# A cached two-layer decode block: the products of each pass in columns, the first pair's q made first, and new tables

## The chip, the cores and the metric

The kernel runs on one core of one Trainium2 chip. The metric is the device time of one execution in microseconds (us), lower is better. A core has a matrix engine (PE, with its weight loads listed apart as PEld), a vector engine (DVE), a scalar engine (ACT), a general engine (POOL) and a sync engine (SP), which here only issues loads. SBUF is the on-chip memory; PSUM holds the results of PE.

## What is computed

Batch 4, one token each, width D = 512, 32 query heads on 8 key and value heads of 128 elements, caches of 4096 positions in bfloat16. Two equal layers run one after the other on the same caches and weights:

```python
def A(x):                                    # attention on the cache
    q = (x @ wq).reshape(B, 1, 32, 128)...
    scores = einsum("bhqd,bhkd->bhqk", q, k) * 128 ** -0.5
    o = einsum("bhqk,bhkd->bhqd", softmax(scores), v)
    return o.reshape(B, 1, 32 * 128) @ wo
def F(x):                                    # gated feed-forward, 1792 wide
    return (sigmoid(x @ w_gate) * (x @ w_up)) @ w_down
x = x + A(layernorm(x)); x = x + F(layernorm(x))
x = x + A(layernorm(x)); x = x + F(layernorm(x))
```

K and V of one batch entry and one head are 1 MB each, so both caches are 64 MB, and each layer needs all of them.

## The kernel before

**Units and pairs.** A unit is one layer, one batch entry and one key head: 64 units. Two neighbouring heads make a pair; `ORDER` (L125) lists the 32 pairs as three digits, layer, batch entry, pair of heads. A batch entry may enter layer 1 as soon as its layer 0 is through, so pairs of both layers are mixed.

**Slots and kept units.** A K or V of a unit takes one of 12 slots in SBUF of 1 MB; the four parts of wq become slots 13 to 16 when q is needed no more (`yield_wq`, L979). `KEPT` (L124) names, for each batch entry, the heads whose K, and behind the slash those whose V, stay in their slots from layer 0 to layer 1; those are loaded once, all others twice. Before, 29 are kept: 19 K and 10 V.

**Loads.** `LOADS` (L129) is the order of all loads: k and v of the next unit, o, g, u, d parts of the four weights besides wq. `pump` (L344) issues them on SP's queue, in that order, each when a slot is free; the new load waits for the last reader of the slot. A K is read last by its scores, a V by its product, unless it is kept.

**Steps.** `PROGRAM` (L133) is the order in which everything else is issued, a letter a step, written out in full. Per pair: T, t, u turn K on DVE in place, whole or by quarters (`k_turn`, L985); b puts q into a block-diagonal tile `qz` (`q_blocks`, L704, four copies on POOL out of `qs`); s and z score the two units on PE (`scores`, L996); m, p, n find the maximum (DVE, PE, DVE); e is exp on ACT; P turns the probabilities on PE; C and D copy them out of PSUM on ACT; h, r, i make the sums; a multiplies by V on PE (`pv`, L1165), o normalises on DVE, w applies wo, and f, F, l turn its row.

**The pass.** The dots of the program are the steps of `pass_steps` (L958), four times 17, one pass for each batch entry between its layers: layernorm, gate and up, down, layernorm, q of layer 1. Before, gate, up and q are made as rows: one column of x is the stationary operand and up to 512 columns of the weights move past it, in four strips of the array, so that the result lies in one row per strip. Gate goes through tanh on ACT as 128x512 (L828), up is multiplied on DVE as 128x512 (L853), `h_turn` (L860) brings the row into columns with four matmuls and a copy; `down` (L929) has its weights stationary. q's two halves go through a 128x512 operation on ACT (L901) and one on DVE (L907), `q_turn` (L912) brings them into columns, `q_spread` (L677) spreads them over the array's rows with 16 matmuls and a copy on ACT into `qs`. Only then may the batch entry's first pair of layer 1 take its b.

The final feed-forward, behind the last pair, has all four entries together, with weights stationary in gate and up.

Of the kernel before, what the change touches and what calls it, by code (L numbers as in the profile page):

```python
# [6 lines left out]
ACTF = mybir.ActivationFunctionType  # L7
# [116 lines left out]
KEPT = ["012345/23", "0145/01", "067/0167", "234567/36"]  # L124
ORDER = """  # L125
002 000 001 003 011 013 101 012 010 102 100 021 022 020 023 110 112 030 103 120 123 032 033 031 113
# [7 lines left out]
stzwbmtpnwett szbwtmh srwPtCTipDaazabnmeaPotthw sttprznwbCmDieaaaawhPoDritpxwttCnetaw szhwbPamTpan  # L134
saDeorwtfuiCaPhuFaazwwalDowmr.Cp.ne.h.i..rP....aa...aaCoiD..aa..tubwu szawxbmapneT
sPhoriCzDaTamabapun szePbmph szoCunbDreiamtahaaor spxPwTinzCwmbDfaewpFawlawanxothPwrit
s.zCehrDmbptta...atun s..uPt.atz..eaoCb. sDhia.raaam..ptoPtCDzwwnei.m.aabwt.paaPohrtCw.un
szimuDabape sznhwbrmPaapoew sizCDPnaamhaaeruhoCipwaDPwaaafubCnDrFloiweahaTawa.oT
sr.PDiw.zmC.apwtbwwna.t.aehao.ri sPCDT...zaawmapne....PahtuoriC.auD.a.baw sztb smpnwzatbmehroTP
spnDziCeaaTPamThprb snaoCzDeiaThamwPabaorittC sDapwznaeaatPmbhptor  # L140
swDiCneaaPhaTarCozmwwiDfapbaFlanaowTeh.rTP sDC.i..z.mb.paa.an.te.thwar.PTo
s..izm..tCD.wa.wpn.eaabaht szboPDCmprneiw szmbapa sThwPnzarteba szoihCDPbmptnaaCraae
sTDhwoiPmpaanCerawaDohziPmaCaparDneaowwihfPFaaClarawDXaoaiNYawa
# [3 lines left out]
def bass_interleave_layers__gqa_block_cached__glu_gated_glu__decode_kernel(  # L147
# [556 lines left out]
    def q_blocks(g):  # L704
        _, b, u = seq[2 * g]
        for a in range(4):
            ps = slice(32 * a, 32 * a + 32)
            S.inst(
                "pool",
                (lambda a, ps: lambda e: e.tensor_copy(  # L710
                    qz_sb[ps, :, :, a, :],
                    qs_sb[b][ps, :, u * REP:(u + 2) * REP].rearrange("p t (u r) -> p u t r", r=REP),
                ))(a, ps),
                reads=[f"qs{b}", "pf"],
                writes=[f"qz{a}"],
            )
# [91 lines left out]
    def gate_row(part):  # L808
        fns = []
        wv = wg_sb.rearrange("p k (f d) -> p k f d", d=2 * P)  # L810
        for k in range(2 * part, 2 * part + 2):
            for st in range(4):
                nt = (KW - st + 3) // 4
                fns.append(
                    (lambda k, st, nt: lambda e: e.matmul(
                        M_ps[0][32 * st:32 * st + 1, 0:nt * 2 * P],
                        lhsT=xc_bf[:, k, 0:1],
                        rhs=wv[:, k, bass.ds(st, nt, step=4), :],
                        start=(k == 0),
                        stop=(k == KD - 1),  # L820
                    ))(k, st, nt)
                )
        if part == 0:
            S.group("pe", fns, reads=["xcb"] + wkeys["wg"], writes=["M0"])
            return
        S.last_write["M0"] = S.group("pe", fns, reads=["xcb"] + wkeys["wg"])
        act(
            lambda e: e.activation(t_row[:, :], M_ps[0][:, :], ACTF.Tanh, scale=rs[:, 0:1]),  # L828
            reads=["rs", "M0"],
            writes=ROW,  # L830
        )

    def up_row(part):
        fns = []
        wv = wu_sb.rearrange("p k (f d) -> p k f d", d=2 * P)
        for k in range(2 * part, 2 * part + 2):
            for st in range(4):
                nt = (KW - st + 3) // 4
                fns.append(
                    (lambda k, st, nt: lambda e: e.matmul(  # L840
                        M_ps[1][32 * st:32 * st + 1, 0:nt * 2 * P],
                        lhsT=xc_bf[:, k, 0:1],
                        rhs=wv[:, k, bass.ds(st, nt, step=4), :],
                        start=(k == 0),
                        stop=(k == KD - 1),
                    ))(k, st, nt)
                )
        if part == 0:
            S.group("pe", fns, reads=["xcb"] + wkeys["wu"], writes=["M1"])
            return  # L850
        S.last_write["M1"] = S.group("pe", fns, reads=["xcb"] + wkeys["wu"])
        dve(
            lambda e: e.scalar_tensor_tensor(  # L853
                out=row_sb[:, 0, :], in0=t_row[:, :], scalar=1.0, in1=M_ps[1][:, :], op0=ALU.add, op1=ALU.mult
            ),
            reads=["rc", "rd", "rb", "M1"],
            writes=["ra"],
        )

    def h_turn():  # L860
        fns = []
        for t in range(2):
            for e_ in range(2):
                fns.append(
                    (lambda t, e_: lambda e: e.matmul(
                        M_ps[0][:, bass.ds(8 * t + e_, 4, step=2)],
                        lhsT=row_sb[:, 0, bass.ds(2 * P * t + e_, P, step=2)],
                        rhs=strips,
                        start=True,
                        stop=True,  # L870
                    ))(t, e_)
                )
        S.group("pe", fns, reads=["ra"] + IDENT, writes=["M0"])
        dve(
            lambda e: e.tensor_copy(hT_bf[:, :, 0], M_ps[0][:, 0:KF]),
            reads=["M0"],
            writes=["rc", "rd"],
        )

    def q_row(h, part):  # L880
        fns = []
        wv = wq_sb.rearrange("p k (h j s d) -> p k h j s d", h=2, j=4, s=4)
        for k in range(2 * part, 2 * part + 2):
            for st in range(4):
                fns.append(
                    (lambda k, st: lambda e: e.matmul(  # L886
                        M_ps[h][32 * st:32 * st + 1, :],
                        lhsT=xc_bf[:, k, 0:1],
                        rhs=wv[:, k, h, :, st, :],
                        start=(k == 0),  # L890
                        stop=(k == KD - 1),
                    ))(k, st)
                )
        rd = ["xcb"] + [f"wq{k}" for k in range(KD)]
        if part == 0:
            S.group("pe", fns, reads=rd, writes=[f"M{h}"])
            return
        S.last_write[f"M{h}"] = S.group("pe", fns, reads=rd)
        if h == 0:
            act(  # L900
                lambda e: e.activation(row_sb[:, 0, :], M_ps[0][:, :], ACTF.Copy, scale=rs[:, 0:1]),  # L901
                reads=["M0", "rs"],
                writes=["ra"],
            )
        else:
            dve(
                lambda e: e.tensor_scalar(row_sb[:, 1, :], M_ps[1][:, :], rs[:, 0:1], None, op0=ALU.mult),  # L907
                reads=["M1", "rs"],
                writes=["rc", "rd", "rb"],
            )  # L910

    def q_turn():  # L912
        fns = []
        for h in range(2):
            for j in range(4):
                n = 4 * (4 * h + j)
                fns.append(
                    (lambda h, j, n: lambda e: e.matmul(
                        M_ps[0][:, n:n + 4], lhsT=row_sb[:, h, j * P:(j + 1) * P], rhs=strips, start=True, stop=True
                    ))(h, j, n)  # L920
                )
        S.group("pe", fns, reads=ROW + IDENT, writes=["M0"])
        dve(
            lambda e: e.tensor_copy(qT_sb[:, 0:HQ], M_ps[0][:, 0:HQ]),
            reads=["M0"],
            writes=["rb"],
        )
# [30 lines left out]
    def pass_steps(b0):  # L958
        return [
            lambda: ln_a(b0, 1, 0.5 * RS),  # L960
            lambda: ln_b(1),
            lambda: gate_row(0),
            lambda: gate_row(1),
            lambda: up_row(0),
            lambda: up_row(1),
            h_turn,
# [469 lines left out]

    ln_a(0, Bn, RS)
# [10 lines left out]
    last = {}  # L1448
    for g in range(NP):
        last[seq[2 * g][:2]] = g  # L1450
    firsts = {}
    for g in reversed(range(NP)):
        firsts[seq[2 * g][:2]] = g
    renewed = set()
    turns = [i for i in range(NU) if loaded("k", i)][2:]
# [6 lines left out]
    def step(c):  # L1462
# [18 lines left out]
        elif c == ".":  # L1481
# [3 lines left out]
            if len(passes) == 2:  # L1485
                yield_wq()
        else:
            g = count[c]
            count[c] += 1
            if c == "b":  # L1490
                l, b, _ = seq[2 * g]
                assert count["z"] == g and (l == 0 or b in renewed)
# [171 lines left out]
```

## Time and profile before

| | us |
|---|---|
| runs: median (lowest to highest, 3 runs) | 306.57 (305.49 to 306.58) |
| the profiled execution | 307.3 |
| its span, first to last instruction | 305.4 |
| output issued in it at | 303.1 |
| mean granted clock of PE | 0.70 |

The loads in the profiled execution:

| load | issues | KB each | median us from issue to landing |
|---|---|---|---|
| V to slots 1 to 12 | 50, and 2 halves | 1024, 512 | 9.5, 23.8 |
| K to slots 1 to 12 | 43 | 1024 | 9.7 |
| V, K to the parts of wq | 3, 2 | 1024 | 10.2, 13.0 |
| wq | 2 | 2048 | 9.9 |
| wo | 8 | 512 | 17.1 |
| gate, up | 2, 2 | 896 | 12.3, 14.2 |
| down | 1, 1 | 1024, 768 | 14.6, 16.1 |

A row of the groups by line reads: line, engine, operation, output<-input, its shape, how often; then busy time in all and mean ns of one; then the idle time of the engine just ahead of it and what ended most of it. Matmuls overlap, so busy time divided by the count is the spacing, and the mean the length of one. A row of the stages has start and end, length, and busy time of PE, PEld, DVE, ACT and POOL with counts, then the granted clock (1 is full), the share of the DMA engines and GB/s. A row of the queue's waits has who waited, for whom, the total, the times and the longest. L12 is line 12 of the kernel; from line 704 on the changed kernel has other line numbers.

### The profile page before, as it was taken

Reading aid. Unit: us, or ns where it says so; the run is one execution under the profiler, and the core shown is the slowest. Engines: PE = TensorE matmul, PEld = TensorE weight load, DVE = VectorE, ACT = ScalarE, POOL = GpSimd, SP = SyncE. Lnnn points to the kernel's source line nnn. Section 1 sums busy time; section 2 is a strip of 40 time slices with the busy share of each in tenths; the row PEclk is TensorE's granted clock in tenths of the full one; section 3 lists DMA queues with packets and bytes.
Section 4 is the critical chain, followed back from the end, with each engine's and each line's share of the span. In section 5 each row is a group of like instructions: output and inputs, shape, how many; then the busy total and the mean of one; then the engine's idle time right before and its main releaser. Section 6 shows DMA issues by size and latency. Waiting matters only on the chain. (4 is left out here: it accounts for less than half of the span.)

```text
span 305.4 us, 11330 instructions
## 1 busy us (share of the span) xinstructions
PE 221.1 (72%) x4872; PEld 150.0 (49%) x4872; DVE 192.6 (63%) x419; ACT 117.6 (39%) x413; POOL 40.3 (13%) x205
## 2 busy tenths in 40 slices
PE   1222451854789788898886789977889798897986
PEld 1221131532645455646555656544647564564675
DVE  6334857377133786786863488649995878484343
ACT  1001142244223245814445634315555424555600
POOL 0001111110000221111121110022211010330000
PEclk9999999999995555756679555565555577555555
DMA  7999999999999999999999999999999999999900
GB/s 292 420 400 418 408 406 391 422 418 407 397 406 417 421 420 414 415 418 421 414 411 412 415 361 422 417 398 420 422 418 417 410 381 384 420 423 420 397 36 3
DMA packets 20505, 118.43 MB, mean 388 GB/s; under 512 B 1892, under 2 KB 5992, under 8 KB 7656
## 3 DMA queue, kind: packets, MB, share of 16 engines
q1 hardware_dynamic: 20432, 117.71, 94.8%
q8 instruction: 38, 0.62, 0.8%
q14 instruction: 11, 0.09, 0.1%
q10 hardware_dynamic: 24, 0.01, 0.0%
HBM read 117.71 MB, written 0.00 MB: 385 GB/s over the span
## 5 line engine op out<-in xcount | busy, mean ns | idle before, releaser
L994 DVE STREAM_TRANSPOSE slot<-slot 128x1024 f32<-128x1024 f32 (+2 forms) x74 | 103.8, 1405 | 19.3 <-DMA slot<-in_A_k_cache_dram 17.1
L1134 ACT ACTIVATE pT<-PT 32x128 bf16<-32x128 f32 x232 | 62.0, 267 | 56.5 <-PE PT L1082 31.8
L1010 PE MATMUL S_ps<-slot,qz 128*16 128x256 bf16 x992 | 61.2, 397 | 14.6 <-DVE slot L994 7.1
L1180 PEld LDWEIGHTS O_ps<-pT,slot 128*128 128x128 bf16 x1792 | 53.2, 103 | 36.7 <-ACT pT L1134 20.9
L1180 PE MATMUL O_ps<-pT,slot 128*128 128x4 bf16 x1792 | 58.3, 166 | 17.3 <-ACT pT L1134 5.9
L1064 ACT ACTIVATE wide<-S_ps,small 128x256 bf16<-128x256 f32 x64 | 30.3, 474 | 56.1 <-DVE small L1057 32.0
L710 POOL COPY qz<-qs 32x32 bf16<-32x32 bf16 x128 | 26.0, 203 | 137.3 <-PE S_ps L1010 71.3
L1010 PEld LDWEIGHTS S_ps<-slot,qz 128*16 128x16 bf16 x992 | 27.0, 112 | 33.8 <-DVE slot L994 9.4
L1027 DVE TENSOR_REDUCE small<-S_ps 128x2 bf16<-128x512 f32 x32 | 21.7, 678 | 16.8 <-PE S_ps L1010 16.0
L1082 PE MATMUL PT<-ident_bf,wide 128*128 128x64 bf16 (+1 forms) x288 | 18.5, 226 | 3.3 <-ACT wide L1064 2.2
L1082 PEld LDWEIGHTS PT<-ident_bf,wide 128*128 128x128 bf16 x288 | 15.1, 121 | 10.2 <-ACT wide L1064 4.6
L1050 DVE SCALAR_TENSOR_TENSOR O_ps<-O_ps,small,wide 128x128 f32<-128x128 f32 x32 | 10.9, 340 | 11.8 <-PE O_ps L1036 9.8
L1237 PE MATMUL AC<-wo,oT 128*1 128x512 bf16 x96 | 11.2, 560 | 7.0 <-DMA wo<-in_A_wo_dram 6.7
L1093 POOL CAST small<-small 128x2 bf16<-128x2 f32 x32 | 5.9, 184 | 79.0 <-ACT wide L1064 71.9
L1211 DVE TENSOR_TENSOR oT<-O_ps,small 128x8 bf16<-128x8 f32 (+1 forms) x32 | 5.4, 167 | 16.1 <-PE O_ps L1180 14.3
L886 PE MATMUL M_ps<-wq,small 128*1 128x512 bf16 x128 | 13.4, 562 | 0.0
L1064 ACT ACTIVATION_READ_ACCUMULATOR wide<-S_ps,small 128x1 f32 x64 | 12.3, 193 | 0.0
L1057 DVE TENSOR_REDUCE small<-O_ps 128x2 f32<-128x128 f32 x32 | 9.3, 292 | 3.3 <-DVE O_ps L1050 0.5
L695 ACT ACTIVATE qs<-M_ps 128x128 bf16<-128x128 f32 x8 | 1.9, 280 | 24.2 <-PE M_ps L684 24.1
L901 ACT ACTIVATE t_row<-M_ps,small 128x512 bf16<-128x512 f32 x4 | 2.7, 687 | 19.6 <-PE M_ps L886 19.6
L1036 PE MATMUL O_ps<-ident_bf,small 128*128 128x64 bf16 x64 | 8.6, 225 | 2.0 <-DVE small L1027 1.6
L1148 PE MATMUL O_ps<-small 128*128 128x4 bf16 x124 | 7.8, 168 | 2.8 <-POOL small L1096 2.6
(144 smaller groups left out, 210.6 us busy)
## 6 DMA issues: line engine op xcount, KB each, us to landing
slot<-in_A_v_cache_dram SPq DMA_DIRECT2D x50, 1024.0 KB, 9.5
slot<-in_A_k_cache_dram SPq DMA_DIRECT2D x43, 1024.0 KB, 9.7
wq<-in_A_wq_dram SPq DMA_DIRECT2D x2, 2048.0 KB, 9.9
wo<-in_A_wo_dram SPq DMA_DIRECT2D x8, 512.0 KB, 17.1
wq<-in_A_v_cache_dram SPq DMA_DIRECT2D x3, 1024.0 KB, 10.2
wq<-in_A_k_cache_dram SPq DMA_DIRECT2D x2, 1024.0 KB, 13.0
wu<-in_B_w_up_dram SPq DMA_DIRECT2D x2, 896.0 KB, 14.2
wg<-in_B_w_gate_dram SPq DMA_DIRECT2D x2, 896.0 KB, 12.3
```

The costliest lines, as they stand in the source:

```text
L710: (lambda a, ps: lambda e: e.tensor_copy(qz_sb[ps, :, :, a, :], qs_sb[b][ps, :, u * REP:(u + 2) * REP].rearrange("p t (u r) -> p u t r", r ...
L886: (lambda k, st: lambda e: e.matmul(M_ps[h][32 * st:32 * st + 1, :], lhsT=xc_bf[:, k, 0:1], rhs=wv[:, k, h, :, st, :], start=(k == 0), sto ...
L994: dve(lambda e: e.transpose(kf, kf), writes=[f"s{st}"])
L1010: (lambda t, b2, e_, c, x1, r0: lambda e: e.matmul(S_ps[p][r0:r0 + 4 * REP, half], lhsT=qz_sb[:, part, t, :, :].rearrange("p a r -> p (a r)"),
L1027: dve(lambda e: e.tensor_reduce(rm_bf, S_ps[p].rearrange("p (u n) -> p u n", u=2), AX.X, ALU.max), reads=[f"S{p}"], writes=["rmb"])
L1050: lambda e: e.scalar_tensor_tensor(out=shifted, in0=maxima, scalar=rowk_f, in1=mask_f.rearrange("p n w -> p (n w)").unsqueeze(1).broadcast ...
L1057: dve(lambda e: e.tensor_reduce(nm_sb, shifted, AX.X, ALU.min), reads=[f"O{n}"], writes=["nm"])
L1064: (lambda u, half: lambda e: e.activation(pe_sb[:, half], S_ps[p][:, half], ACTF.Exp, bias=nm_sb[:, u:u + 1], scale=exp_scale, accum_out=s ...
L1082: (lambda w, a0, a1, c0: lambda e: e.matmul(PT[:, c0:c0 + 16 * (a1 - a0)], lhsT=wide_sb[:, NV + 64 * w:NV + 64 * w + P], rhs=valid_bf[:, : ...
L1134: (lambda dst, frm: lambda e: e.activation(dst, frm, ACTF.Copy))(dst, frm),
L1180: (lambda n, x, c, j: lambda e: e.matmul(bank[:, ul * REP:(ul + 1) * REP], lhsT=vv[:, x * JG + c * 4 + j, :], rhs=pT[:, x % 2, ul, j, 2 * ...
L1237: (lambda r, h, i: lambda e: e.matmul(AC[32 * r:32 * r + 1, :], lhsT=oT_sb[:, h, own_column:own_column + 1], rhs=wo_sb[:, h, :], start=(j ...
```

## The change

- `KEPT` names 32 units instead of 29: 20 K and 12 V. `LOADS` has 110 entries instead of 113, with another order; `ORDER` and `PROGRAM` are other tables of the same kind.
- Gate and up of a pass are made in columns, 56 matmuls each with a 128x128 block of the weights stationary and one column of x moving, as `down` was already. Tanh and the product then work on 14 columns (128x14), and `h_turn` is gone; an empty step stands in its place.
- q of a pass is made in columns too, 128 matmuls in four groups of 32 (8 heads, two key heads each). The group of the entry's first pair of layer 1 comes first, is scaled on DVE, spread by 16 matmuls, and the pair's step b copies it from PSUM into `qz`, two of four copies on DVE and two on ACT. The other three groups follow, then the scale and spread of all heads into `qs`, from which later pairs take their blocks on POOL as before. So there are two spreads a pass, and each pass still has 17 steps.
- wq's parts become slots when one step of the last pass is left, not two; that is behind the last q matmul in both.

```diff
-KEPT = ["012345/23", "0145/01", "067/0167", "234567/36"]
+KEPT = ["012345/023", "0145/015", "0167/0167", "234567/67"]
 ORDER = """
-002 000 001 003 011 013 101 012 010 102 100 021 022 020 023 110 112 030 103 120 123 032 033 031 113
+003 001 002 000 011 013 101 012 010 100 102 021 022 110 023 020 112 103 030 123 032 120 031 033 113
 111 121 133 131 130 132 122
 """
 LOADS = """
-vkookkvkkk ovkovkoovk ukvkvkvogo guddvvvkvk kkvkvvvkvk kvkkvvvkvk vvvvvvkkkv vkvvkvvkvk kkvkkkkvvv
-vkkvvkkkvv kvvkkvvvvv vvv
+kokkkkookk ouvkkkoovo vvkkvovvvg gdudvvkkvv kkvvkvvkvk kvvkkvvkvv kvkvkvvvkk vvkvvkkkvv kkkvvkvvkk
+vkkvvkvvkv kvkvvvvvvv
 """
...
     def q_blocks(g):
-        _, b, u = seq[2 * g]
+        l, b, u = seq[2 * g]
+        if l == 1 and g == firsts[1, b]:
+            frm = M_ps[1][:, 0:NT4 * HQ].rearrange("p (t h) -> p t h", t=NT4)[:, :, u * REP:(u + 2) * REP]
+            frm = frm.rearrange("p t (u r) -> p u t r", r=REP)
+            for a in (0, 2, 1, 3):
+                ps = slice(32 * a, 32 * a + 32)
+                if a < 2:
+                    dve(
+                        (lambda a, ps: lambda e: e.tensor_copy(qz_sb[ps, :, :, a, :], frm[ps]))(a, ps),
...
+                else:
+                    act(
+                        (lambda a, ps: lambda e: e.activation(qz_sb[ps, :, :, a, :], frm[ps], ACTF.Copy))(a, ps),
...
+            return
...
+    def inner_columns(w_sb, M, mk, wk, part):
         fns = []
+        for fc in range(KW * part, KW * part + KW):
+            for k in range(KD):
                 fns.append(
+                    (lambda fc, k: lambda e: e.matmul(
+                        M[:, 64 + fc:65 + fc],
+                        lhsT=w_sb[:, k, bass.ds(fc // 2 * 2 * P + fc % 2, P, step=2)],
+                        rhs=xc_bf[:, k, 0:1],
...
+    def gate_columns(part):
+        inner_columns(wg_sb, M_ps[0], "M0", "wg", part)
+        if part == 1:
+            act(
+                lambda e: e.activation(t_sb[:, 0:KF], M_ps[0][:, 64:64 + KF], ACTF.Tanh, scale=rs[:, 0:1]),
...
+    def up_columns(part):
+        inner_columns(wu_sb, M_ps[1], "M1", "wu", part)
+        if part == 1:
+            dve(
+                lambda e: e.scalar_tensor_tensor(
+                    out=hT_bf[:, :, 0], in0=t_sb[:, 0:KF], scalar=1.0, in1=M_ps[1][:, 64:64 + KF],
...
+    def q_columns(n, first):
         fns = []
+        for h in range(2 * REP * n, 2 * REP * (n + 1)):
+            for k in range(KD):
                 fns.append(
+                    (lambda h, k: lambda e: e.matmul(
+                        M_ps[0][:, h:h + 1],
+                        lhsT=wq_sb[:, k, h * DH:(h + 1) * DH],
+                        rhs=xc_bf[:, k, 0:1],
...
+    def q_scale(h0, h1):
+        dve(
+            lambda e: e.tensor_scalar(qT_sb[:, h0:h1], M_ps[0][:, h0:h1], rs[:, 0:1], None, op0=ALU.mult),
...
+    def spread_of(h0, h1):
...
+                        M_ps[1][32 * a:32 * a + 32, t * HQ + h0:t * HQ + h1],
+                        lhsT=ident_bf[:, bass.ds(c0, 32, step=2)],
+                        rhs=qT_sb[:, h0:h1],
...
     def pass_steps(b0):
...
             lambda: ln_a(b0, 1, 0.5 * RS),
             lambda: ln_b(1),
-            lambda: gate_row(0),
-            lambda: gate_row(1),
-            lambda: up_row(0),
-            lambda: up_row(1),
-            h_turn,
+            lambda: gate_columns(0),
+            lambda: gate_columns(1),
+            lambda: up_columns(0),
+            lambda: up_columns(1),
+            lambda: None,
             lambda: down(b0, 1, 0),
             lambda: down(b0, 1, 1),
             lambda: ln_a(b0, 1, RS),
             lambda: ln_b(1),
-            lambda: q_row(0, 0),
-            lambda: q_row(0, 1),
-            lambda: q_row(1, 0),
-            lambda: q_row(1, 1),
-            q_turn,
-            lambda: (q_spread(b0, 1), renewed.add(b0)),
+            first_q,
+            first_spread,
+            lambda: q_columns(rest[0], True),
+            lambda: q_columns(rest[1], False),
+            last_q,
+            all_spread,
         ]
...
-            if len(passes) == 2:
+            if len(passes) == 1:
                 yield_wq()
```

More of the change, by code (lines that the diff above doesn't have):

```diff
@@ L844, in up_row @@
                         start=(k == 0),
                         stop=(k == KD - 1),
-                    ))(k, st, nt)
+                    ))(h, k)
                 )
[L848 to L851, printed above, removed]
-        dve(
[L853 to L857, printed above, removed]
+        rd = ["xcb"] + [f"wq{k}" for k in range(KD)]
@@ L869, in h_turn @@
                         start=True,
                         stop=True,
-                    ))(t, e_)
+                    ))(t, a, 64 * b2 + e_)
                 )
[L873 to L927, printed above, removed]
+        S.group("pe", fns, reads=["rb"] + IDENT, writes=["M1"])
@@ L1435, in last_unit @@
         parts(sq_hl, sq_sb.rearrange("p k b -> p (k b)"), ["rd"], "rb")
+    last = {}
+    for g in range(NP):
+        last[seq[2 * g][:2]] = g
+    firsts = {}
+    for g in reversed(range(NP)):
+        firsts[seq[2 * g][:2]] = g
     ln_a(0, Bn, RS)
```

107 lines of the change are left out of this document (56 added, 51 removed).

## The prediction

> **What bounds the kernel now.** I read the page first, for how full the transfers are and when they end.
>
> ```profile
> span 305.4 us, 11330 instructions
> PE 221.1 (72%) x4872; PEld 150.0 (49%) x4872; DVE 192.6 (63%) x419; ACT 117.6 (39%) x413; POOL 40.3 (13%) x205
> ...
> DMA  7999999999999999999999999999999999999900
> GB/s 292 420 400 418 408 406 391 422 418 407 397 406 417 421 420 414 415 418 421 414 411 412 415 361 422 417 398 420 422 418 417 410 381 384 420 423 420 397 36 3
> ...
> q1 hardware_dynamic: 20432, 117.71, 94.8%
> q8 instruction: 38, 0.62, 0.8%
> ```
>
> The DMA engines are busy in 38 of 40 slices; no compute engine is over 72%. The span is one stream of 117.71 MB, a short start and a tail. To see where the stream is not full, I then read the stages:
>
> ```profile
> 10.00:90.00 80.00, 37.88 (x796) 24.62 (x797) 41.62 (x70) 19.93 (x72) 7.38 (x37) 1.00 1.03 408
> 90.00:170.00 80.00, 66.93 (x1500) 44.55 (x1497) 54.33 (x122) 37.40 (x132) 14.23 (x71) 0.64 1.01 416
> 170.00:180.00 10.00, 7.56 (x202) 6.62 (x200) 5.95 (x11) 3.93 (x14) 0.61 (x3) 0.50 0.93 371
> 180.00:240.00 60.00, 51.86 (x1099) 34.43 (x1096) 45.13 (x84) 29.08 (x103) 9.74 (x49) 0.53 1.01 417
> 240.00:260.00 20.00, 18.13 (x357) 11.29 (x358) 16.81 (x41) 7.07 (x24) 2.31 (x12) 0.67 1.00 386
> 260.00:290.00 30.00, 26.08 (x557) 17.20 (x555) 15.49 (x31) 17.48 (x65) 5.69 (x29) 0.50 1.01 416
> ```
>
> Columns after the length: PE, PE weight load, DVE, ACT and POOL busy, granted clock, DMA share, GB/s. A full stream of 1 MB loads moves 416 GB/s, so one load of 1.0486 MB costs 2.52 us. Only 170 to 180 and 240 to 260 fall below: 10 x (416 - 371) / 416 = 1.1 us and 20 x (416 - 386) / 416 = 1.4 us, 2.5 us together. So **bytes bound the time**, and the rest is a question of slots. The queue's own waits say who gives it slots, and the loads' line how long a load takes:
>
> ```profile
> SPq L106 <- PE O_ps L1180: 99.4, 40, 12.1
> SPq L106 <- PE S_ps L1010: 47.7, 19, 7.4
> ```
>
> ```profile
> DMA to landing us min/median/max: 5.9/9.7/24.2
> ```
>
> The load queue waits for scores (L1010) and for probabilities times V (L1180), which free slots. A load issued onto an empty stream lands 5.9 us later; the last ones wait 24.2 us behind others, so at the end the stream, not a slot, is late.
>
> **The change, part by part.** *Fewer loads.* 29 kept units become 32, so the load table falls from 113 entries to 110, three loads of 1.0486 MB: 3 x 2.52 = **-7.6 us**. Everything else in the stream is the same bytes. The tail behind the last landing holds the same code.
>
> *Tighter slots.* Three more slots stand still between the layers. I followed the program's order and waits in both kernels and asked for each load whose data must have arrived before the step that frees its slot. Where that is the load k places earlier, the new one is in time if 2.52 x k covers the turnaround plus 5.9 us: 1.7 us of turnaround for k = 3, 4.2 us for k = 4. Before, one load has k = 3 and 20 have k = 4; after, six (numbers 37, 38, 41, 42, 70 and 96 of the table, counted from 0) and 20. What a turnaround takes is in the timeline and in the loads' line at one place:
>
> ```profile
> 92.15 1.02 PE L1180 MATMUL O_ps<-pT,slot 128*128 128x4 bf16 x32
> ```
>
> ```profile
> 93.25 0.33 SPq L370 DMA_DIRECT2D slot<-in_A_v_cache_dram  x1
> ```
>
> A V that PE waits for is used in 1.02 us and the next load goes out at its end, 1.1 us after the start. All six are of this kind, so each fits, barely. A K has to be turned on DVE first (103.8 + 4.8 us for 45 of them, 2.4 us each, rows below) and then scored (1 us), 3.5 us. The price of one that is late, by the one load of before with k = 3, and what moved around it:
>
> ```profile
> L370 SPq DMA_DIRECT2D slot<-in_A_v_cache_dram x1: 328/328/328, 159.3 to 159.3; - x1
> ```
>
> ```profile
> 158.00:162.00 4.00, 3.55 (x117) 3.12 (x121) 2.35 (x7) 1.59 (x6) 1.60 (x8) 1.00 0.97 379
> ```
>
> 4 x (416 - 379) / 416 = 0.36 us are missing. Five more such loads cost nothing if they all fit, 5 x 0.36 = 1.8 us at that row, and 5 x (3.5 + 5.9 - 7.6) = 9 us if PE turns them no faster than a K. I take **+1.8 us**, the row of the same case; the ends 0 and 9 stay.
>
> *The pass.* These rows carry its old and its nearest new operations:
>
> ```profile
> L994 DVE STREAM_TRANSPOSE slot<-slot 128x1024 f32<-128x1024 f32 (+2 forms) x74 | 103.8, 1405 | 19.3 <-DMA slot<-in_A_k_cache_dram 17.1 <-PE S_ps L1010 1.6
> ...
> L710 POOL COPY qz<-qs 32x32 bf16<-32x32 bf16 x128 | 26.0, 203 | 137.3 <-PE S_ps L1010 71.3 <-ACT qs L695 47.5 <-PE M_ps L815 4.2
> ...
> L886 PE MATMUL M_ps<-wq,small 128*1 128x512 bf16 x128 | 13.4, 562 | 0.0
> ...
> L840 PE MATMUL M_ps<-wu,small 128*1 128x512 bf16 (+1 forms) x64 | 8.2, 547 | 0.0
> L815 PE MATMUL M_ps<-wg,small 128*1 128x512 bf16 (+1 forms) x64 | 8.1, 567 | 0.0
> ...
> L935 PE MATMUL M_ps<-t_row,wd 128*128 128x1 bf16 x224 | 6.4, 164 | 1.3 <-DMA wd<-in_B_w_down_dram 0.7 <-DVE t_row L875 0.6
> ...
> L994 DVE STREAM_TRANSPOSE wq<-wq 128x1024 f32<-128x1024 f32 (+1 forms) x3 | 4.8, 1593 | 0.2 <-DMA wq<-in_A_k_cache_dram 0.2
> ...
> L656 PE MATMUL M_ps<-small,wq 128*128 128x4 bf16 x128 | 3.6, 166 | 5.9 <-DMA wq<-in_A_wq_dram 5.9
> ...
> L907 DVE TENSOR_SCALAR t_row<-M_ps,small 128x512 bf16<-128x512 f32 x4 | 3.0, 752 | 1.9 <-PE M_ps L886 1.9
> ...
> L901 ACT ACTIVATE t_row<-M_ps,small 128x512 bf16<-128x512 f32 x4 | 2.7, 687 | 19.6 <-PE M_ps L886 19.6
> L853 DVE SCALAR_TENSOR_TENSOR t_row<-t_row,M_ps 128x512 bf16<-128x512 f32 x4 | 2.7, 686 | 2.7 <-ACT t_row L828 1.7 <-PE M_ps L840 0.9
> L828 ACT ACTIVATE t_row<-M_ps,small 128x512 f32<-128x512 f32 x4 | 2.7, 685 | 8.1 <-DVE small L536 7.7 <-DVE small L1027 0.4
> ...
> L695 ACT ACTIVATE qs<-M_ps 128x128 bf16<-128x128 f32 x8 | 1.9, 280 | 24.2 <-PE M_ps L684 24.1
> L684 PE MATMUL M_ps<-t_row,ident_bf 128*32 128x32 bf16 (+1 forms) x80 | 1.8, 212 | 11.0 <-DVE t_row L667 10.4 <-DVE t_row L924 0.6
> ...
> L918 PE MATMUL M_ps<-ident_bf,t_row 128*128 128x4 bf16 x32 | 1.4, 169 | 0.2 <-DVE t_row L907 0.2
> ```
>
> Column matmuls come at 6.4 / 224 = 28.6 ns (L935, one moving column) or 3.6 / 128 = 28.1 ns (L656). On PE a pass loses gate 8.1 / 4 = 2.0, up 2.05, q 3.35 and q's turn 1.4 / 4 = 0.35, together 7.8 us (h's turn left out); it gains 56 + 56 columns, 3.2 us, 128 columns of q, 3.6, and a second spread of 16 matmuls, at most 16 x 1.8 / 80 = 0.36: 7.2 us. So -0.6 us per pass, -2.4 of 221 us in all. On DVE and ACT four 128x512 operations per pass (0.69, 0.69, 0.69, 0.75) give way to small ones; a PSUM read of 14 or 32 columns has its nearest rows in
>
> ```profile
> L1126 DVE CAST slot<-PT 32x128 bf16<-32x128 f32 x4 | 1.2, 293 | 0.1
> ...
> L875 DVE CAST t_row<-M_ps 128x14 bf16<-128x14 f32 x4 | 0.7, 180 | 1.0 <-PE M_ps L865 0.9
> ```
>
> that is 0.18 to 0.29 us each; I take 0.2. The turn-round of a batch gets shorter: from q to its first block 3.35 + 0.75 + 0.35 + 0.18 + 0.36 + 0.28 + 4 x 0.2 = 6.1 us become 32 columns 0.9, scale 0.2, spread 0.36, and two copies on each of two engines 0.4, 1.9 us; gate to h loses some 2 us more. None of this is on the path that ends, which is the stream; it gives time to slots that wait for layer 1, and that is what the three more kept units spend. I cost it at nothing. If that cover is gone (PE late everywhere), it is worth 2.4 us at most.
>
> *Added waits.* The first pair's four copies move from POOL to DVE and ACT, behind the 16 spread matmuls; what stands behind them is the next K's turn and maximum on DVE and the copies of probabilities on ACT, for under 0.9 us (the 32 columns) a pass. Before, DVE stood 1.9 us in all for q at L907, so this hides as it did. The remaining blocks stay on POOL, 13% busy. 180 more matmuls and weight loads a pass are 1440 instructions, 13% more than 11330: 13% of the 0.8% of the span that instructions take on the queues, **+0.3 us**.
>
> *The clock.* The scores run at either clock:
>
> ```profile
> 157.00:167.00 10.00, 2.60 (x76) 1.62 (x68) 1.00 1.01 408
> 260.00:285.00 25.00, 10.54 (x160) 4.65 (x160) 0.50 1.01 420
> ```
>
> 34 ns each at full clock, 66 at half, 6.4 of them a us. By the stages above (0.64, 0.53, 0.67) about 33 us behind 90 us are at full clock. [...]
>
> **Sum.** Against the profiled execution, 307.3 us (span 305.4): -7.6 + 1.8 + 0.3 = -5.5, 301.8 us. That execution is 0.7 above the median of the runs, 306.57; against the median it is **301.1 us**.
>
> **Rivals.** *Slots starve the stream (slower).* If PE comes to the six V loads 3.5 us after they land and not 1.1, the term is 9: -7.6 + 9 + 0.3 = +1.7 us, 308.3. It decides from a turnaround of 1.7 us. For it: in 240 to 260, where six loads in a row have k = 4, the stream already loses 1.4 us. Against it: the six are all V, and PE is idle over a quarter of the span.
> *The clock stays low.* 33 us hold at most 33 x 6.4 score matmuls, each 32 ns dearer: 6.8 us of PE. Half of it on the path gives 301.1 + 3.4 = 304.5, all of it 307.9. Against it: PE is not the path. [...]
> *More than the bytes.* The dip of 240 to 260 has the last pass's q rows in it:
>
> ```profile
> 240.00:260.00 20.00, 3.26 (x32) 0.89 (x32) 0.67 1.00 386
> ```
>
> If the shorter pass closes it (1.4 us) and the six loads fit, -7.6 - 1.4 + 0.3 = -8.7, 297.9; with the other dip closed too, 296.8. Against it: there too six loads in a row have k = 4 or less after the change.
>
> **How the numbers follow.** Forecast (299 to 303) 0.55; more than the bytes, below 299, 0.12; low clock or more starving, 303 to 305, 0.15; starving that eats the gain, 305 to 308.1, 0.09; slots starve, above, 0.09. A measurement can tell about 0.5%, 1.5 us: faster 0.82, the same 0.09, slower 0.09. The range 297.5 to 306.2 leaves out about 0.07 below and 0.11 above.
>
> **What would show it.** 114.56 MB read; the stream ending some 5.5 us earlier and the tail unchanged; DMA at 410 or more GB/s but for short dips near loads 37 to 42, 70 and 92 to 99; q columns near 28 ns. Wrong: several more slices under 390 GB/s, a shortest landing still 5.9 us but many of them near it, or the last PV waiting for ACT and not for its V.

## The result and the profile after

The changed kernel takes **315.46 us** (313.57 to 316.33, 4 runs), the kernel before in the same comparison 306.03 (305.47 to 306.58, 4 runs): ratio 1.030, 95% interval 1.0246 to 1.0354. It is 9.4 us slower where 301.1 us were forecast, and outside the range. The profiled execution of after took 315.22 us, with a span of 313.3.

The page of after: busy times, GB/s in 40 slices, the data and instruction queues, and the chain that ended last.

```profile
span 313.3 us, 12749 instructions
PE 224.7 (72%) x5592; PEld 169.8 (54%) x5592; DVE 187.8 (60%) x420; ACT 115.2 (37%) x417; POOL 37.1 (12%) x189
...
GB/s 298 407 421 393 407 418 381 418 407 421 405 415 394 348 352 415 397 383 410 394 379 354 419 292 325 334 385 362 342 423 422 379 350 391 382 419 422 410 55 3
...
q1 hardware_dynamic: 20000, 114.57, 93.0%
q8 instruction: 44, 0.72, 0.9%
...
PE 46%; DMA 20%; DVE 11%; SPq 9%; issue 9%; ACT 2%; POOL 1%; DVEq 0%; POOLq 0%
```

The bytes fell as forecast, by three loads. But the stream is no longer full: over a dozen slices lie under 385 GB/s, and PE carries 46% of the chain that ends last. The same stages as before, with the same columns:

```profile
10.00:90.00 80.00, 36.87 (x852) 26.34 (x853) 40.38 (x66) 20.24 (x74) 7.37 (x37) 1.00 1.03 407
90.00:170.00 80.00, 69.29 (x1746) 52.84 (x1749) 50.56 (x121) 33.22 (x122) 11.41 (x57) 1.00 0.98 384
170.00:180.00 10.00, 8.28 (x175) 5.06 (x167) 7.17 (x11) 6.51 (x24) 1.37 (x7) 1.00 1.02 413
180.00:240.00 60.00, 48.57 (x1222) 37.49 (x1222) 39.20 (x81) 25.73 (x94) 8.19 (x42) 1.00 0.95 358
240.00:260.00 20.00, 16.54 (x427) 13.23 (x420) 15.57 (x32) 5.75 (x21) 2.24 (x11) 1.00 0.96 374
260.00:290.00 30.00, 26.30 (x663) 19.06 (x661) 19.46 (x44) 16.29 (x61) 5.37 (x27) 1.00 1.01 405
```

Up to 90 us hardly anything changed (408 and 407 GB/s). Behind it the stream lost 80 x (416 - 384) / 416 = 6.2 us, then 60 x (416 - 358) / 416 = 8.4 us, then 2.0 and 0.8: 17.4 us, where before lost 2.5. These 15 us are most of the 17.0 that make a loss of 9.4 out of a gain of 7.6. (The granted clock stands at 1.00 here because this execution recorded no change of the clock before 288 us. From 90 to 290 us its 832 score matmuls were busy for 52.64 us, 63 ns each, near the 66 ns that the prediction's rows give at half clock, so that 1.00 is not to be taken at its word.)

What the slots wait for is in the load queue's own waits of after. Those for scores come to 80.3 us in all:

```profile
SPq L106 <- PE S_ps L1009: 51.8, 18, 7.2
...
SPq L370 <- PE S_ps L1009: 28.5, 14, 5.0
```

Before, they were 47.7 and 16.5 us, 64.2 in all. Those for the products with V hardly changed, 102.1 and 103.1 us.

What PE waited for between 90 and 300 us, after (total us, times, longest), where "issue" is time in which it waited for nothing that the profile shows:

```profile
PE M_ps L870 <- issue: 6.0, 6, 1.8
PE O_ps L1179 <- issue: 5.8, 7, 1.4
PE S_ps L1009 <- issue: 2.6, 2, 1.4
...
PE M_ps L913 <- issue: 1.9, 2, 1.2
```

and before:

```profile
PE O_ps L1180 <- DMA slot<-in_A_v_cache_dram: 4.8, 6, 1.0
PE S_ps L1010 <- issue: 2.4, 2, 1.9
...
PE O_ps L1180 <- issue: 1.3, 3, 0.8
```

Before, PE stood 3.7 us for "issue" in this stretch; the largest of its waits in total was the one for V, 4.8 us. After, it stood 17.9 us (all lines together), in 21 pieces of 0.9 us on average and up to 1.8 us, some of them in the middle of a run of equal matmuls. Its waits for everything else shrank from 25.8 to 14.5 us. The chain of after in order of time shows one such piece, within q's columns (start, length, what):

```profile
98.86 0.20 PE M_ps L870 x4
99.06 1.25 issue
100.30 0.89 PE M_ps L870 x28
```

And the groups by line of after that answer to the rows of the prediction:

```profile
L1009 PE MATMUL S_ps<-slot,qz 128*16 128x256 bf16 x992 | 63.1, 408 | 12.8 <-DVE slot L993 4.9 <-POOL qz L728 4.5 <-issue 2.6
...
L870 PE MATMUL M_ps<-small,wq 128*128 128x1 bf16 x512 | 17.0, 165 | 6.1 <-issue 6.0
...
L831 PE MATMUL M_ps<-small,wg 128*128 128x1 bf16 x224 | 7.0, 165 | 0.2 <-issue 0.2
...
L886 DVE TENSOR_SCALAR t_row<-M_ps,small 128x8 bf16<-128x8 f32 (+1 forms) x8 | 1.9, 239 | 6.9 <-PE M_ps L870 6.9
```

q's columns are busy for 17.0 / 512 = 33 ns each, not 28, and the stops are not in that. They follow one another as forecast, though: the 28 columns of the chain take 0.89 us, and without the length of the last one, 165 ns, that is 27 ns from one to the next. The 512 stand in 22 pieces in the trace, and each piece ends with the length of a whole matmul.

### The profile page after: what moved, and what is told of

It is laid out like the page before. It is cut to its first block, busy times and chain, and to the rows that moved or that the text cites. A ratio compares the mean times of both kernels' runs of the same rounds, so it can differ in the third digit from the quotient of the medians.

```text
span 313.3 us, 12749 instructions
## 1 busy us (share of the span) xinstructions
PE 224.7 (72%) x5592; PEld 169.8 (54%) x5592; DVE 187.8 (60%) x420; ACT 115.2 (37%) x417; POOL 37.1 (12%) x189
## 3 DMA queue, kind: packets, MB, share of 16 engines
q1 hardware_dynamic: 20000, 114.57, 93.0%
## 4 chain that ended last, share of the span: by engine, by line
PE 46%; DMA 20%; DVE 11%; SPq 9%; issue 9%; ACT 2%; POOL 1%; DVEq 0%; POOLq 0%
PE O_ps L1179 13%; PE S_ps L1009 12%; DMA slot<-in_A_v_cache_dram 10%; DVE slot L993 7%; SPq L370 6%; DMA slot<-in_A_k_cache_dram 5%; DMA wu<-in_B_w_up_dram 5%; PE M_ps L870 5%; PE PT L1081 3%; PE M_ps L831 3%; SPq L350 3%; ACT wide L1063 1%; PE M_ps L913 1%; PE O_ps L1329 1%; PE M_ps L570 1%
## 5 line engine op out<-in xcount | busy, mean ns | idle before, releaser
L993 DVE STREAM_TRANSPOSE slot<-slot 128x1024 f32<-128x1024 f32 (+2 forms) x71 | 101.1, 1427 | 18.9 <-DMA slot<-in_A_k_cache_dram 16.6
L1133 ACT ACTIVATE pT<-PT 32x128 bf16<-32x128 f32 x236 | 63.1, 268 | 72.6 <-PE PT L1081 34.7
L1179 PE MATMUL O_ps<-pT,slot 128*128 128x4 bf16 x1888 | 62.7, 167 | 31.2 <-DMA slot<-in_A_v_cache_dram 14.5
L1179 PEld LDWEIGHTS O_ps<-pT,slot 128*128 128x128 bf16 x1888 | 59.1, 105 | 44.5 <-issue 18.7
L1009 PE MATMUL S_ps<-slot,qz 128*16 128x256 bf16 x992 | 63.1, 408 | 12.8 <-DVE slot L993 4.9
L728 POOL COPY qz<-qs 32x32 bf16<-32x32 bf16 x112 | 22.7, 203 | 99.7 <-PE S_ps L1009 63.0
L1026 DVE TENSOR_REDUCE small<-S_ps 128x2 bf16<-128x512 f32 x32 | 21.7, 677 | 11.4 <-PE S_ps L1009 11.3
L1210 DVE TENSOR_TENSOR oT<-O_ps,small 128x8 bf16<-128x8 f32 (+1 forms) x32 | 5.4, 170 | 27.5 <-PE O_ps L1179 25.8
L870 PEld LDWEIGHTS M_ps<-small,wq 128*128 128x128 bf16 x512 | 15.9, 105 | 10.0 <-issue 10.0
L870 PE MATMUL M_ps<-small,wq 128*128 128x1 bf16 x512 | 17.0, 165 | 6.1 <-issue 6.0
L1049 DVE SCALAR_TENSOR_TENSOR O_ps<-O_ps,small,wide 128x128 f32<-128x128 f32 x32 | 11.1, 346 | 12.6 <-PE O_ps L1035 11.3
L1236 PE MATMUL AC<-wo,oT 128*1 128x512 bf16 x96 | 12.3, 620 | 0.2 <-DVE oT L1210 0.2
L913 PE MATMUL M_ps<-t_row,wd 128*128 128x1 bf16 x224 | 7.0, 165 | 2.3 <-issue 1.9
```

The source lines that it names most:

```text
L728: (lambda a, ps: lambda e: e.tensor_copy(qz_sb[ps, :, :, a, :], qs_sb[b][ps, :, u * REP:(u + 2) * REP].rearrange("p t (u r) -> p u t r", r ...
L870: (lambda h, k: lambda e: e.matmul(M_ps[0][:, h:h + 1], lhsT=wq_sb[:, k, h * DH:(h + 1) * DH], rhs=xc_bf[:, k, 0:1], start=(k == 0), stop= ...
L993: dve(lambda e: e.transpose(kf, kf), writes=[f"s{st}"])
L1009: (lambda t, b2, e_, c, x1, r0: lambda e: e.matmul(S_ps[p][r0:r0 + 4 * REP, half], lhsT=qz_sb[:, part, t, :, :].rearrange("p a r -> p (a r)"),
L1026: dve(lambda e: e.tensor_reduce(rm_bf, S_ps[p].rearrange("p (u n) -> p u n", u=2), AX.X, ALU.max), reads=[f"S{p}"], writes=["rmb"])
L1049: lambda e: e.scalar_tensor_tensor(out=shifted, in0=maxima, scalar=rowk_f, in1=mask_f.rearrange("p n w -> p (n w)").unsqueeze(1).broadcast ...
```

## The experiments

Two theories stood at the start. **A**: PE became what the stream waits for, with its waits and its stops; the slots come free late because PE is late. **B**: the three more kept units leave too few slots (the rival "Slots starve the stream"). Later A was split into **T** (PE's busy time counts) and **F** (the supply of PE's instructions counts: they come in packets, 44 with 0.72 MB on the page of after, and PE stops when the next one is not there yet). Times are medians; the kernel before stood at 305.9 to 306.6 us beside them.

### The tables and the code apart

`cols_old_tables`: columns in the pass, on before's tables; the first pair takes its q like all others.

```diff
-KEPT = ["012345/023", "0145/015", "0167/0167", "234567/67"]
+KEPT = ["012345/23", "0145/01", "067/0167", "234567/36"]
...
-        if l == 1 and g == firsts[1, b]:
+        if False:
```

> Columns alone, on the tables of before: 29 kept units, gate, up and q of each pass in columns, all blocks of q out of qs as before. Theory of instructions (A: the columns add some 1300 instructions on PE; PE stands inside its bursts until the next 16 KB of them have come in, and in the middle of the run PE is what everything waits for): 310 to 316 us, with more stops of 0.4 to 2 us inside PE's bursts than before. Theory of slots (B: three more kept units leave too few slots for the stream): 305 to 307 us, since the slots are those of before.

Measured: 319.18 us (318.4 to 320.76), ratio 1.041 (1.0374 to 1.0445). With the old number of kept units, nothing of B is in it, and it is slower still, above A's range too. PE stood 22.1 us for "issue" from 90 to 300 us, most of it here:

```profile
PE O_ps L1176 <- issue: 11.0, 8, 2.6
PE M_ps L870 <- issue: 5.7, 4, 2.6
```

`rows_new_tables`: before's code on after's tables, with the last dots of each pass moved ahead of the first pair's b.

> The other half: gate, up and q in rows as before, on the tables of after with 32 kept units; the last three or four steps of each pass are put ahead of the first pair's q block, which in rows needs all of q. A: 300 to 306 us, as PE has before's instructions and 3 MB less are loaded. B: 312 to 318 us, as the slots are those of after.

Measured: 320.12 us (318.86 to 320.35), ratio 1.044 (1.0406 to 1.0475). A expected a gain, so this speaks against A as I had put it; B's range ends at 318, and the trace shows another loss: from 90 to 120 us, where the first pass lies,

```profile
90.00:120.00 30.00, 22.90 (x473) 14.21 (x477) 15.82 (x37) 11.02 (x38) 4.23 (x21) 0.54 0.84 316
```

the stream has 316 GB/s (418 in before), and behind 90 us PE waits longest for q's blocks (2.2 us in before):

```profile
PE S_ps L1010 <- POOL qz L710: 7.0, 6, 1.5
```

Either mix is slower than both kernels, so the two halves of the change can't be summed from these two runs.

### Slots or PE

`two_less_kept`: after with two V fewer kept, thus two loads more and more free slots.

```diff
-KEPT = ["012345/023", "0145/015", "0167/0167", "234567/67"]
+KEPT = ["012345/23", "0145/01", "0167/0167", "234567/67"]
...
```

> After, with two of the 32 kept units given up (V of two heads, loaded a second time at their place in the order): 30 kept, 2.1 MB more to load, two slots freed between the layers. A: 314 to 319 us, no better, as PE's work is the same and the loads are 5 us longer. B: 307 to 311 us, as the stream has room again.

Measured: 316.92 us (315.89 to 319.19), ratio 1.0354 (1.0303 to 1.0406). B expected 307 to 311 and falls as the one cause. The two loads more are 5.0 us of stream, and the run is only 1.5 us longer; whether the freed slots gave back part of that or the stream had room for it, this run does not tell.

`less_q`: after, with q of the other 24 heads made from k = 0 alone.

```diff
-            for k in range(KD):
+            for k in range(KD if n == n0 else 1):
...
```

> After, with three quarters of the sum left out for the 24 heads of q that are not the first pair's in each pass (one of four blocks of 128 is multiplied, so 72 of 128 columns fall away a pass): 288 matmuls and weight loads fewer, 8 us of PE at 28 ns, and about two instruction fetches. A, or PE in any other way: 303 to 309 us. B: 313 to 316 us, the slots are the same.

Measured: 307.61 us (304.97 to 309.53, 8 runs), ratio 1.003 (0.9992 to 1.0068). With 288 pairs of weight load and matmul taken from PE (busy for 214.6 us, after 224.7), 7.9 us of the 9.4 are back:

```profile
PE 214.6 (70%) x5304; PEld 160.5 (52%) x5304; DVE 187.2 (61%) x420; ACT 115.4 (37%) x417; POOL 37.1 (12%) x189
```

No slot, load or order is changed: A holds.

`less_q_gu`: in addition k = 0 alone for gate and up.

```diff
-            for k in range(KD):
+            for k in range(1):
...
```

> The kernel after with k = 0 alone for q's other 24 heads and for gate and up of each pass (not the reference's values): 624 pairs fewer, 1248 PE instructions and 17.5 us of PE. The prediction's own sum, if PE is out of the way: bytes bound it and the three loads fewer show, 299 to 302 us. By the prices of the runs so far (12 ns an instruction, 0.4 of the PE time) it would come to 293 and is held at that floor. If slots or the order of the tables still starve the stream, 303 to 307, near the 307.6 of the run with q alone cut.

Measured: 300.70 us (300.27 to 301.55), ratio 0.980 (0.9752 to 0.9842). Its page and its stretch from 90 to 290 us:

```profile
PE 207.2 (69%) x4968; PEld 153.3 (51%) x4968; DVE 186.5 (62%) x420; ACT 115.1 (39%) x417; POOL 37.1 (12%) x189
...
q1 hardware_dynamic: 20000, 114.57, 95.5%
```

```profile
90.00:290.00 200.00, 165.32 (x4000) 122.85 (x3997) 135.71 (x305) 92.85 (x339) 29.37 (x147) 0.60 0.99 397
```

With 17.5 us less on PE, the same bytes, slots and tables give what was forecast, 5.9 us less than before. So the gain is in the new tables, and the pass's work on PE keeps it away. PE is lighter here than even in before (221.1 us), so the run does not say that after could have it whole.

### Busy time or number of instructions

`less_q_wide`: less_q, with PE time put back as 84 wide matmuls.

```diff
+            for i in range(7):
...
+                        M_ps[0][32 * (i % 4):32 * (i % 4) + 1, 64:512],
+                        lhsT=xc_bf[:, i % KD, 0:1],
+                        rhs=wq_sb[:, i % KD, 0:448],
```

> The kernel after without three quarters of the column matmuls of q's other 24 heads (k = 0 alone is left, so q of these heads is not the reference's; 288 pairs of weight load and matmul fewer, some 8 us of PE, as in the run that took 307.6), but with their PE time put back as 21 wide matmuls a pass (one column of x stationary, 448 columns moving, about 91 ns each, 7.6 us in all) into unused PSUM columns. Theory T, PE time: PE's busy time is what the stream waits for, so the 7.9 us that the shorter run won are lost again: 313 to 316 us. Theory F, instruction supply: PE's instructions come in packets of 16 KB of about 256, one every 6 us beside the loads, and what costs is the number of instructions; only 168 are put back for the 576 taken: 306 to 310 us.

Measured: 310.77 us (309.52 to 311.98), ratio 1.0143 (1.0095 to 1.0192).

```profile
PE 226.1 (73%) x5388; PEld 163.8 (53%) x5388; DVE 187.7 (61%) x420; ACT 115.4 (37%) x417; POOL 37.4 (12%) x189
```

PE is busier than in after (226.1 against 224.7 us), yet the kernel is 4.7 us faster, with 408 PE instructions fewer. Busy time does not explain that; the number of instructions fits it, and so do the stops: PE stood 13.0 us for "issue" from 90 to 300 us, 4.9 less than in after. The time lies between the two ranges. Of the 7.9 us, 3.2 came back, but with the busy time came 168 instructions. At less_q's price, 7.9 us for 576 instructions or 14 ns each, these would make 2.3 of the 3.2 us, so this run doesn't settle whether busy time counts by itself.

`before_cols_more` and `before_wide_more`: before, with 96 column or 26 wide matmuls more a pass.

```diff
+        for i in range(24 * (part == 0)):
...
+                    lhsT=wq_sb[:, i % KD, 0:P],
+                    rhs=xc_bf[:, i % KD, 0:1],
```

```diff
+        for i in range(6 * (part == 0)):
...
+                    lhsT=xc_bf[:, i % KD, 0:1],
+                    rhs=wq_sb[:, i % KD, 0:512],
```

> The kernel before with 96 column matmuls more a pass (24 each ahead of gate, up and the two halves of q, into PSUM columns that are overwritten afterwards; the output is the reference's): 384 pairs, 768 PE instructions, 10.8 us of PE at 28 ns. What I predicted (PE is not the path) would give 306 to 308. Theory T, PE time: PE was a second bound behind 90 us, so 310 to 317, and the same as the run with wide matmuls. Theory F, instruction supply: three more packets of 6 us, 18 us of supply, part of it in slack: 309 to 318, and clearly more than with wide matmuls.

> The kernel before with 26 matmuls of 512 moving columns more a pass, at the same places: 104 of them, 208 PE instructions, 10.8 us of PE at 104 ns; the output is the reference's. What I predicted (PE is not the path): 306 to 308. Theory T, PE time: 310 to 317, within 1.5 us of the run with 96 columns more. Theory F, instruction supply: under one packet more: 306 to 309, several us below that run.

Measured: columns 317.87 us (316.8 to 318.7), ratio 1.0384 (1.0331 to 1.0438); wide 310.46 us (309.33 to 312.42), ratio 1.014 (1.0084 to 1.0196). PE busy, columns first:

```profile
PE 233.8 (74%) x5256; PEld 160.8 (51%) x5256; DVE 192.6 (61%) x419; ACT 117.8 (37%) x413; POOL 40.7 (13%) x205
```

```profile
PE 225.1 (73%) x4976; PEld 151.4 (49%) x4976; DVE 192.2 (62%) x419; ACT 117.8 (38%) x413; POOL 40.7 (13%) x205
```

I had meant both to add 10.8 us. They added 12.7 and 4.0: the rows of the wide ones hold 16.5 us, so they overlap other matmuls, and the scores took 59.6 us instead of 61.2. So this pair doesn't tell T from F: the kernels lost 11.7 and 4.2 us, about what PE gained, and also 15 and 20 ns for each added instruction. T had both within 1.5 us and F the wide ones under 309, and both missed. But the pair shows the step that failed: in the kernel *before*, more work on PE already showed at about the full length of its busy time.

`before_less_down` takes 40 pairs a pass from before.

```diff
-            for k in range(KF):
+            for k in range(4):
```

> The kernel before with 4 of the 14 k of down in each pass (not the reference's values): 160 pairs fewer, 320 PE instructions and 4.6 us of PE. If bytes alone bound before, as I predicted: 305.5 to 306.5. If before already pays for PE and its instructions in part (the dips at 170 to 180 and 240 to 260 us): 303 to 305.

Measured: 305.61 us (304.63 to 306.93), ratio 0.9969 (0.9943 to 0.9994), 1.0 us faster. PE is busy for 217.1 us there, 4.0 less. Less PE gains next to nothing in before, as the prediction had it; more costs at once. That fits a kernel that stood where the stream and PE meet.

### The supply of instructions by itself

`supply_12`: a kernel of its own, 1536 column matmuls without loads, 1536 beside loads of 1 MB, up to 12 at once, then 480 wide ones; `supply_3` has at most 3 at once. The core of both:

```diff
+    alone = columns(1536, 0)
+    for n in range(60):
...
+    columns(1536, 1, deps=[first])
+    wide(480, 0)
```

> A kernel of its own that leaves out the whole computation (its output is x): 1536 column matmuls (weight load 128x128 and one moving column, as in q's columns) on PE with no load under way; then 60 loads of 1 MB, up to 12 at once, and beside them, from the first landing, 1536 column matmuls again and then 480 matmuls of 512 moving columns. Theory F, instruction supply: alone some 28 ns a pair, 43 us; beside the loads 256 PE instructions every 6 us, 47 ns a pair, 72 us, with stops; the wide ones 104 ns both ways, 50 us. Theory T, PE time: 28 ns a pair beside the loads too, 43 us, no stops over 0.3 us.

> The same with at most 3 loads at once. If the instruction packets wait behind the loads that stand in the queues, theory F expects them to come sooner: 28 to 40 ns a pair beside the loads; if they only share the engines' bandwidth, the same 47 ns as with 12. Theory T: 28 ns.

The stretches of supply_12, without loads, columns beside loads, wide beside loads (PE, PE weight load and POOL busy, clock, DMA share, GB/s):

```profile
14.00:54.00 40.00, 38.84 (x1429) 38.53 (x1427) 0.00 (x0) 1.00 0.02 5
70.00:130.00 60.00, 35.25 (x1276) 34.70 (x1275) 0.00 (x0) 1.00 1.01 420
140.00:160.00 20.00, 20.00 (x376) 8.20 (x372) 0.00 (x0) 1.00 1.01 418
```

Alone, PE is busy 97% of the time; beside the loads 59%; with wide matmuls again all the time. The chain beside the loads:

```profile
62.67 6.08 PE M_ps L185 x222
68.75 2.21 issue
70.96 3.55 PE M_ps L185 x128
74.51 2.64 issue
...
86.63 3.19 issue
89.82 3.55 PE M_ps L185 x128
93.37 2.65 issue
```

128 pairs, that is 256 instructions, in 3.55 us (28 ns a pair), then a stop, over and over. From 68.75 to 93.37 there are four turns, 6.16 us each: **41.6 PE instructions a microsecond**, where without loads PE ran (1429 + 1427) / 40 = 71.4. The instruction queue agrees: 44 packets (0.72 MB, 16.4 KB each) for the 2 x 5592 PE instructions of after are one for 254, and 38 for the 2 x 4872 of before one for 256. In supply_3, with 3 loads at once,

```profile
69.53 3.56 PE M_ps L185 x128
73.08 2.37 issue
75.45 3.55 PE M_ps L185 x128
```

a turn is 5.92 us, at 414 GB/s from 70 to 130 us. So the number of loads ahead hardly matters. That the full DMA engines slow the packets is then the nearest reading; how they do it is not shown. T expected 28 ns a pair beside the loads and falls here; F's 47 ns are 48. Now the rates of the kernels, 90 to 290 us, before and then after:

```profile
90.00:290.00 200.00, 170.56 (x3699) 114.10 (x3696) 137.71 (x286) 94.95 (x335) 32.58 (x163) 0.58 1.01 411
```

```profile
90.00:290.00 200.00, 168.98 (x4211) 127.68 (x4212) 131.96 (x285) 87.49 (x320) 28.57 (x143) 1.00 0.98 380
```

Before issues (3699 + 3696) / 200 = 37.0 PE instructions a us, after (4211 + 4212) / 200 = 42.1: as many as the supply kernel got beside a full stream. The packets themselves agree: by the trace's records of the instruction queue they start 6.06 us apart on average in after between 90 and 290 us, about as in supply_12, and 6.94 us apart in before, where PE asked for fewer. So F fits after. That T holds beside it is argued, not shown: PE was busy 85% of this stretch in both. (less_q_gu, which ends at 298.5 us, comes to 40.0, under the 41.6 of supply_12; PE stood at most 2.2 us for "issue" at any one line there.)

### Fewer columns on the new tables

`gu_rows` is after with gate and up in rows as before; `q_rows_rest` has q in rows behind the first pair's columns; `few_columns` has both.

```diff
-            lambda: gate_columns(0),
+            lambda: gate_row(0),
...
-            lambda: q_columns(rest[0], True),
-            lambda: q_columns(rest[1], False),
-            last_q,
+            lambda: q_row(0),
+            lambda: q_row(1),
+            q_turn,
```

> The kernel after with gate and up of each pass in rows as before (with h's turn), q as after: 76 pairs fewer a pass, 608 PE instructions in all, against about 0.9 us more PE time a pass and two 128x512 operations longer. Theory T, PE time: 315.5 + 3.6, 317 to 320 us. Theory F, instruction supply: 2.4 packets of 6 us, 14 us less supply: 304 to 310 us.

> The kernel after with q of all heads in rows behind the first pair's columns, gate and up in columns: 56 pairs fewer a pass, 448 PE instructions in all, some 1.0 us more PE time a pass, 4 in all. Theory F: 315.5 - 5.4 + 1.6 = 311.7, 309 to 314. If PE time alone counts, or the tables lose the time: 315 to 319.

> The kernel after with gate and up of each pass in rows (as before) and q of all heads in rows behind the first pair's q, which alone stays in columns: 132 pairs fewer a pass, 1056 PE instructions in all, against some 1.9 us more PE time a pass, 7.6 in all. Theory F, instruction supply, with the prices of the runs so far (12 ns an instruction, 0.4 of the PE time): 315.5 - 12.7 + 3.0 = 305.8; between 300 and 308 it holds. If the tables of after lose the time themselves: 311 to 316.

Measured: 313.65 us (312.04 to 316.67), ratio 1.0249 (1.0178 to 1.032); 318.60 (317.81 to 319.39), ratio 1.0399 (1.0358 to 1.044); 319.08 (316.91 to 320.4), ratio 1.0414 (1.0353 to 1.0475). F with a fixed price for an instruction fails in all three; gu_rows lies below T's range as well, and few_columns above what was expected if the tables lose the time. few_columns, with 1056 PE instructions fewer than after, stands only 6.4 us for "issue" behind 90 us, but now waits for DVE and ACT:

```profile
PE S_ps L1082 <- DVE slot L1066: 4.5, 5, 2.3
...
PE O_ps L1252 <- ACT pT L1206: 3.9, 6, 1.5
...
PE S_ps L1082 <- ACT qz L719: 3.3, 2, 2.0
```

The rows bring back 128x512 operations on DVE and ACT, and PE waits for these two engines, in an order of steps written for columns. That this order is what loses was not tried by itself, for it needs new tables; it stays open. No run here beat the kernel before but those that leave work out.

## Why the prediction was wrong

*Fewer loads, -7.6 us.* Right in the bytes, 114.57 MB. In time, 5.9 us of it showed in less_q_gu (300.70 us), as soon as PE was lighter. That this is so near the forecast of 301.1 is in part luck, since PE is lighter there than in either kernel.

*"None of this is on the path that ends, which is the stream", "I cost it at nothing. If that cover is gone (PE late everywhere), it is worth 2.4 us at most."* This is the step that failed, in its premise and its sign. I read 72% and a full stream as slack on PE. The stages that I quoted had the answer: PE 66.9 of 80 us, 51.9 of 60, 18.1 of 20, 26.1 of 30, that is 84 to 91% behind 90 us (76% in the short dip from 170 to 180), with 3.7 + 25.8 = 29.5 us of waits between 90 and 300 us. before_cols_more and before_wide_more show the price of more work on PE in the kernel before, 0.92 and 1.05 us for each us that PE gained. And PE's sum was not -2.4 but +3.6 us (221.1 to 224.7): q's columns alone took 17.0 us instead of 4 x 3.6 = 14.4.

*"180 more matmuls and weight loads a pass are 1440 instructions ... +0.3 us."* The mis-sized term. I counted the bytes of the instructions, a share of the DMA engines' time; what the runs show beside a full stream is a rate at which they come, 41.6 a microsecond in supply_12. The stops on PE grew by 17.9 - 3.7 = 14.2 us; with the 3.6 us of busy time that is 17.8, against the 17.0 that the result asks for (-7.6 + 17.0 = +9.4). That these agree so well is luck, as PE's waits for other engines and for data shrank by 11.3 us in the same stretch. The runs show that PE's work as a whole makes the loss (less_q, less_q_gu) and that busy time alone doesn't (less_q_wide); each part's share stays open.

*"q columns near 28 ns."* This sign came: 27 ns from one to the next. They are busy for 33 ns each because they stand in 22 pieces; the rows L935 and L656 that gave 28 came in runs of 56 and of 128.

*Tighter slots, +1.8, and the rival "Slots starve the stream", 308.3.* The rival had the right side and the wrong mechanism. Slots were freed late, and two of the signs that I had named for being wrong came: over a dozen slices under 390 GB/s, and 25 of the loads issued from 90 to 270 us landing within 7.5 us, 11 before. But they were freed late because PE was late: less_q_gu, with the same slots and tables, reaches 300.70 us, and two_less_kept, with more slots, is no faster. My turnaround of 1.1 us was taken where PE stood waiting for that V; with PE behind, no slot is freed at once. And 5.9 us was the shortest landing in before, of a load issued at 176.02 us with two others still under way, not onto an empty stream.

*"The clock stays low."* Small: all scores together, those on wq's slots with them, took 64.7 us against 63.6, 1.1 us of PE. No run shows columns to hold the clock low: the three executions of after besides the profiled one have a granted clock of 0.70 to 0.71, the profiled one of before 0.70. *"More than the bytes"*: the dip at 240 to 260 us got deeper, 374 GB/s against 386; that at 170 to 180 us closed, 413 against 371.

*Added waits.* q's scale on DVE waited 6.9 us in all for q's columns, more than the under 0.9 us a pass. It does not show on PE, whose waits for DVE between 90 and 300 us are 9.5 us, 9.6 before.

## What to carry to other kernels

Read how busy an engine is in the stretch that decides, not over the span: 72% was 47% from 10 to 90 us and 85% behind, and in the later part more work on PE cost about its full length (0.92 and 1.05 us for each us). A column matmul is two instructions for 28 ns of work; beside a stream that fills the DMA engines, PE got some 42 instructions a microsecond (41.6 in supply_12, 42.1 in after), so count instructions per microsecond, not their bytes. And a table of steps may serve only the code that it came with: here neither half of the change did any good by itself.

## What the runs showed of the hardware

- PE's instructions came in packets, one for 254 in after and for 256 in before. Beside 420 GB/s of loads PE ran 256 instructions every 6.16 us in supply_12, with a stop of 2.2 to 3.2 us after them (5.92 us in supply_3, with 3 loads at once); without loads 28 ns a pair, with 1.2 us of stops in 40 us.
- After a pause of 6.3 us in supply_12 PE ran 222 pairs, 444 instructions, before its first stop, less than two packets.
- 480 matmuls of 512 columns had no stop beside the loads of supply_12: from 140 to 160 us, at a granted clock of 1.00 and 418 GB/s, a matmul and its weight load take 53 ns (20.00 us for 376), more than the 48 ns in which the supply gives two instructions.
